# An order of work written out by hand, replaced by another: delta-rule attention and a cosine-gated feed-forward layer on one core

## The chip, the core and the metric

The kernel runs on one core of a Trainium2 chip. The metric is the device time of one execution in microseconds (us); before the change the median of three runs is 665.59 us (663.34 to 668.86). The core has five engines that work side by side, each through its own list of instructions in order: TensorE (PE: matrix products; its weight loads are PEld), VectorE (DVE), ScalarE (ACT), GpSimd (POOL) and SyncE (SP). SP does nothing here but issue transfers (DMAs); ACT issues some too, POOL only the first constants.

## The reference

Two blocks follow each other. The first is a delta rule: for each of 4 batches and 8 heads a 48 x 48 state is carried over 768 tokens. The second is a feed-forward layer on the 3072 tokens, 384 wide, with 2048 hidden features and a cosine gate.

```
k_n = k / (norm(k) + 1e-6)
for t in range(768):
    y[t]  = q[t] @ state
    v_old = k_n[t] @ state
    state = state + beta[t] * outer(k_n[t], v[t] - v_old)
x = y, put together to (3072, 384)
h = x @ w_in ;  out = (h * cos(h)) @ w_out
```

## The kernel before, in words

**Units and pairs.** The 768 tokens are cut into 24 units n of 32 tokens. A unit holds 4 batches x 32 tokens = 128 rows of 8 heads. Two units make a stage m of the attention and a pair p of the feed-forward layer (256 tokens); there are 12 of each.

**Attention, per unit.** Keys and queries are loaded (`k`, `q`, line 327) and turned on PE (`turn`, line 535, and `turn_out`, line 545); from unit 8 on `blocks` (line 338) brings the queries and keys for a turn on DVE (line 551). `square`, `sum`, `norms` (line 487, a power on POOL) and `scale` make the factors; `weigh` scales the values `v`. `gram` (line 566) multiplies keys with keys and queries; `gram_keys`/`gram_queries` (lines 577, 600) take it out; `gram_put` (line 618) writes it to memory and, per stage, `gram_get` (line 639) reads it back with other rows, into the one buffer `gb`. Then the 32 x 32 triangles of the stage are inverted by elimination, `inv(m, 0)` to `inv(m, 6)`: pairs of a product (line 676) and a subtraction (line 683), on POOL (on DVE for stage 0). `put` (line 697) and `get` (lines 708, 716) carry the inverse back. On PE follow `state` (line 733), `solve` (line 796; the first two units solve in halves, `solve_half`, `between`, `solve`), `update` (line 819) and `within` (line 836), with `right`, `solve_out`, `update_out`, `within_out` between them on DVE and ACT; `features` (line 855) hands the unit to the feed-forward layer.

**Weights.** They come as 8-byte floats in 28 pieces (`weights`, line 435), and are cut to 4 bytes by `split` (ACT, lines 443, 445), `shift` (DVE, 449, 454) and `add` (POOL, line 458). `hidden(0, f)` needs the pieces up to 3(f/2 % 4 + 1).

**Feed-forward layer, per pair.** Pairs 0 and 1 take a plain first product, `hidden` (line 876). The others take it in a scheme with fewer products: `x_sum` (line 969, POOL) adds and subtracts blocks of the features into 11 combinations named d, n, m, e, k, g, i, l, f, h and b0 (each 128 x 128); `layer(p, j)` (line 1054) multiplies one with a block of weights, 20 for a pair; `layer_out` (lines 1066, 1068, 1071) combines the results on ACT and DVE. `turns`, `rest`, `cos`, `gate` (lines 917, 924, 933, 936) make h cos(h). The second product is plain for pair 0 (`out`, line 1077); the others take seven products in two parts, `out(p, step, part)` (line 1134), with `left` sums (line 1150) and `collect` (line 1186) on DVE, and a `store`.

**What sets the order.** All of this is added as 2083 tasks with their dependencies. The class `Order` then goes through them in the sequence that the string `LINE` gives, a list of task numbers, and writes out each task's instructions; the costs and due times that `add` also takes are not read. The instructions of an engine run in that sequence, and each waits for what it needs of the others. Buffers follow it too: there is one `gb`, one of the PSUM places named `two` and `kq`, three named `h`. Every transfer issued by SP or ACT waits for the one issued eight places before it in the sequence (the semaphores go round in eight).

In `LINE`, near a change from pair p to the next, the first product with combinations is `layer(p, 18)` (it reads d), then `layer(p, 15)` (no combination), then `layer(p, 1)` (g), `layer(p, 4)` and `layer(p, 10)` (i), with parts of `out(p - 1, ...)` and attention products between them.

Of the kernel before, what the change touches and what calls it, by code (L numbers as in the profile page):

```python
# [55 lines left out]
0 1971 1 2 14 10 11 12 3 4 37 5 42 15 72 6 38 7 39 16 43 73 40 1972 13 1975 44 96 17 75 45 19 97  # L56
18 79 76 46 77 1979 1973 20 48 1976 47 1974 78 80 104 1977 99 1983 100 1978 81 49 101 82 50 83 84
105 102 1987 1984 51 132 106 1980 107 9 108 52 22 1991 131 53 1988 36 54 1995 1981 55 56 155 138
1992 1989 1982 1985 109 1990 1996 1999 1993 1986 139 1997 21 1994 134 41 1998 110 135 818 136 2003
2000 23 57 24 111 2001 25 112 26 2007 27 74 2004 822 28 137 2002 156 29 113 2005 30 2011 186 32 31  # L60
140 33 187 2006 141 114 142 2012 2015 34 98 58 35 2013 210 143 115 59 2016 60 2019 211 679 61 116
2020 2023 241 2021 62 680 63 64 117 2027 65 2024 681 2008 66 2017 68 684 69 265 67 189 118 2009
2031 190 159 103 86 160 685 161 2028 162 2018 119 163 682 2029 70 2014 71 87 2035 2032 193 164 686
2010 683 689 194 2033 85 191 687 688 2039 694 690 825 165 2025 2034 243 820 2030 88 166 244 699
695 2026 2043 89 2036 120 2022 696 691 167 697 90 2037 2040 92 2047 698 719 93 296 91 2044 168
2041 700 701 94 121 702 2048 704 122 2051 2042 703 95 133 692 2045 2038 693 709 245 705 706 2055
192 714 710 157 2049 2046 707 711 2050 708 712 195 2059 169 2052 713 747 8 715 188 196 2056 197
2057 123 748 2063 170 720 826 749 212 124 750 2053 125 2064 198 127 716 2067 320 2058 752 819 717
126 128 2054 2060 751 171 718 129 753 757 2061 130 2068 754 2071 755 2069 214 758 756 2062 762 215
2065 2070 298 158 2066 2075 216 759 247 172 767 217 760 299 763 761 2072 764 2079 2076 772 735 248  # L70
2073 765 173 768 766 145 823 219 773 2077 2080 721 774 269 2081 775 731 777 776 2078 218 174 769
220 2082 146 770 2074 782 268 824 778 771 300 779 722 828 221 144 832 783 833 222 739 723 249 725
724 821 302 246 223 743 147 829 303 726 732 148 834 224 175 784 149 837 151 150 351 727 152 830
780 827 225 736 788 153 176 831 154 785 744 728 737 740 741 226 177 270 242 178 729 179 787 323
733 790 213 227 781 180 793 182 375 181 794 183 838 786 184 796 791 185 840 250 798 842 200 228
251 266 252 789 851 742 799 852 730 792 253 353 201 271 800 272 354 274 855 843 801 745 844 802
856 841 738 229 846 797 845 804 267 847 848 859 849 835 850 275 853 860 355 806 734 857 854 301
868 199 276 273 858 807 869 805 861 304 277 866 862 836 872 357 867 746 202 863 870 203 278 864
230 808 873 865 204 839 206 871 406 876 279 205 207 874 809 795 231 875 803 878 232 877 810 280
324 879 894 882 898 895 233 883 297 899 896 880 234 900 811 881 281 897 358 235 902 237 236 884  # L80
812 430 903 886 885 282 904 208 887 814 209 901 238 325 888 239 815 889 240 905 379 910 954 255
923 953 906 955 816 890 960 907 961 378 408 962 892 911 956 908 922 957 893 958 912 909 959 305
817 283 913 321 918 964 891 968 924 965 306 914 925 307 308 969 919 326 409 920 966 327 813 256
972 329 967 410 921 928 970 915 929 322 971 284 973 979 963 916 931 980 917 330 930 983 933 974
926 331 254 934 927 359 935 285 984 332 981 936 987 413 982 937 411 988 975 932 985 333 412 328
939 976 977 257 941 986 991 258 334 989 992 259 1011 261 260 461 993 262 990 942 1012 335 938 1013
995 940 943 1014 1007 286 944 994 1008 945 336 287 978 946 352 356 996 288 1015 947 999 1009 289
949 337 1010 1016 290 1000 376 1017 292 291 1019 997 948 263 1020 998 485 338 950 380 1021 1001
264 951 293 1003 1002 294 1022 1035 295 1018 1023 1038 1024 1066 360 1004 1041 1068 1025 1005 1069
339 1067 434 1076 1042 1006 1070 361 1073 1031 1077 362 1074 1036 463 1075 1081 1072 1032 363 1078  # L90
1071 381 1026 1082 310 382 1033 383 1027 384 464 1079 1034 1085 465 377 1083 1086 1080 1044 1028
1084 1037 1094 1029 385 1046 1092 1095 309 1087 1030 1093 1039 386 1098 1088 311 952 1096 340 1040
1047 1089 387 1097 1090 1048 1099 1091 312 1102 313 388 1100 414 314 1101 1049 316 468 1043 1104
317 1103 389 315 1050 433 1105 1052 466 1124 1120 341 516 1121 1106 390 342 1122 1108 1054 1107
343 1109 1125 1055 1123 344 1128 467 1110 391 1126 1045 1056 1111 1127 345 1057 347 540 346 1114
1051 392 1112 1129 318 1113 1058 1130 1115 319 1131 1059 348 1136 1053 407 349 1132 1060 393 1118
1137 350 1062 1133 1061 1138 435 1134 1063 1139 489 415 1119 365 1064 1144 1135 518 1116 1179 416
1181 1145 1148 1182 1117 394 1186 1146 418 366 1190 1180 1140 1183 469 1194 1185 1184 1151 417
1195 1189 1141 1187 1147 1188 1198 1142 1149 436 364 1199 1150 1196 1154 1191 437 1143 1207 439
519 1192 1152 1155 520 1193 488 438 1197 1157 1156 1205 1159 440 1153 367 1206 1158 395 1200 368  # L100
1209 1201 1208 522 1160 441 1210 1202 1211 442 1203 1213 1065 523 1161 1204 1214 1212 1217 521 443
431 1215 1218 369 1162 1237 1216 371 571 370 1163 1233 372 444 1234 1165 1238 1164 396 1239 1167
1235 1221 397 490 1168 445 1222 1236 544 1219 1240 398 1220 1223 399 1241 462 1169 1242 446 400
1170 1243 402 1224 401 595 1225 432 1227 373 1226 447 1171 374 1244 403 1228 1245 1172 1166 486
1249 404 1173 1229 405 1246 1231 1250 1292 1174 1294 543 1175 573 1232 1295 1296 1247 1303 1297
574 1293 1176 1302 1304 1262 1298 1251 1248 448 1307 1177 1257 1305 1230 470 1306 1258 420 1308
471 1259 472 1261 421 1260 1264 524 1178 1253 1299 473 575 1252 491 1267 1263 1309 449 492 1268
1254 1310 494 1300 1255 1313 1301 1311 576 578 1314 1318 1312 1256 1270 1265 1319 1266 495 496
1320 1271 419 1322 1272 1315 1273 1323 1316 450 1321 1274 1324 497 1275 577 1317 1326 1269 1276
1327 493 487 1330 498 422 1325 1331 1278 423 1350 1328 1351 424 499 1329 1352 426 626 425 1332  # L110
# [80 lines left out]
def kernel(  # L191
# [159 lines left out]
    near = 132 + C  # L351
# [516 lines left out]
    gates, p_hs, turns, rests, p_os, outs = ({} for _ in range(6))  # L868
# [326 lines left out]
    def store(p, i, cols=slice(0, DM)):  # L1195
# [12 lines left out]
            x=2, x_sum=XS, turns=2, g=GATES, o=2, o_out=2,  # L1208
# [3 lines left out]
    add = order.add  # L1212
# [480 lines left out]
```

## Time and profile before

| | |
|---|---|
| median of three runs | 665.59 us |
| profiled execution: its time / its span | 668.13 us / 666.3 us |
| PE busy / instructions | 604.3 us (91%) / 11960 |
| DVE, POOL, ACT busy | 487.5, 448.5, 261.4 us |
| mean granted TensorE clock | 0.978 |
| DMA: bytes / mean rate | 51.78 MB / 78 GB/s |

The page's second part cuts the span into 40 slices and gives the busy share of each engine in tenths; PEclk is the clock that TensorE was granted. The chain (fourth part) goes back from the last instruction to what released it, step by step. A line of the timeline gives start, duration, engine, source line, operation and tiles, and in brackets the idle time before it and what ended that.

### The profile page before, as it was taken

What the parts mean: (1) busy time and instruction counts of PE and PEld (TensorE: products, weight loads), DVE (VectorE), ACT (ScalarE), POOL (GpSimd) and SP (SyncE); (2) the same over time, 40 slices, a digit from 0 to 9 for tenths busy, and PEclk for the clock granted to TensorE, in tenths of its full rate; (3) what the DMA queues carried; (4) which work ended last, traced back from release to release, by engine and by line L of the source; (5) the groups of instructions that cost most, each with busy time, mean ns of one, the idle gap of its engine ahead of it and who ended that gap; (6) DMA issues with size and microseconds to landing.
All of it is one profiled execution on the core that took longest, in us unless ns stands there. A gap on an engine that the chain in (4) does not pass through costs nothing.

```text
span 666.3 us, 27542 instructions
## 1 busy us (share of the span) xinstructions
PE 604.3 (91%) x11960; PEld 565.6 (85%) x11960; DVE 487.5 (73%) x886; ACT 261.4 (39%) x446; POOL 448.5 (67%) x844
## 2 busy tenths in 40 slices
PE   4317689999989999989999999999999999999997
PEld 3216578896789999989999999998999999999996
DVE  5784275989868888768978778867668678566782
ACT  3432364662123533523533534523334434336340
POOL 4378766888898878858858858968658679403000
PEclk9999698999989999989999999999999999999999
DMA  8875674566353553343453352541421410200000
GB/s 179 195 168 121 157 162 110 129 122 104 58 98 50 77 99 58 55 80 53 78 101 56 72 87 40 93 74 27 72 59 29 86 21 14 47 3 25 1 25 25
DMA packets 215644, 51.78 MB, mean 78 GB/s; under 512 B 207076, under 2 KB 210420, under 8 KB 215524
## 3 DMA queue, kind: packets, MB, share of 16 engines
q1 hardware_dynamic: 204516, 43.39, 35.4%
q10 hardware_dynamic: 10752, 6.20, 3.7%
q8 instruction: 94, 1.54, 1.0%
q0 software_dynamic: 256, 0.44, 0.3%
q14 instruction: 26, 0.21, 0.1%
HBM read 39.24 MB, written 10.75 MB: 75 GB/s over the span
## 4 chain that ended last, share of the span: by engine, by line
PE 45%; POOL 32%; DMA 9%; issue 6%; DVE 4%; ACT 1%; SPq 1%; ACTq 0%; POOLq 0%; DVEq 0%
PE p_out L1134 17%; PE p_h L1054 16%; POOL z L683 13%; POOL part L676 13%; POOL x_sum L969 4%; PE p_h L876 3%; DMA gb<-g_dr 3%; DMA qp<-in_q_dram 2%; PE p_kq L733 2%; PE p_u L796 2%; PE p_o L1134 2%; PE p_s L819 1%; PE p_kq L836 1%; DMA zt<-z_dr 1%; PE p_out L1077 1%
## 5 line engine op out<-in xcount | busy, mean ns | idle before, releaser
L676 POOL TENSOR_TENSOR part<-z,gb 128x126 f32<-128x126 f32 (+22 forms) x341 | 148.8, 436 | 66.6 <-DMA gb<-g_dr 27.0
L683 POOL TENSOR_TENSOR z<-z,part 128x126 f32<-128x126 f32 (+22 forms) x341 | 157.5, 462 | 26.7
L1134 PE MATMUL p_out<-w_out,g_ffn 128*128 128x192 f32 x672 | 120.1, 327 | 0.0
L1134 PEld LDWEIGHTS p_out<-w_out,g_ffn 128*128 128x128 f32 x672 | 107.9, 190 | 0.5
L933 ACT ACTIVATE turns<-turns,halfpi 128x512 f32<-128x512 f32 x96 | 68.7, 721 | 61.3 <-DVE turns L924 60.7
L1134 PE MATMUL p_out<-w_sum,g_ffn 128*128 128x192 f32 x496 | 91.3, 332 | 0.8 <-DVE o L1186 0.8
L1054 PE MATMUL p_h<-x_sum,w_in 128*128 128x128 f32 x640 | 85.5, 282 | 4.2 <-POOL x_sum L969 3.4
L1054 PEld LDWEIGHTS p_h<-x_sum,w_in 128*128 128x128 f32 x640 | 79.2, 195 | 6.0 <-POOL x_sum L969 3.8
L1134 PEld LDWEIGHTS p_out<-w_sum,g_ffn 128*128 128x128 f32 x496 | 80.7, 193 | 1.7 <-DVE o L1186 1.0
L917 ACT ACTIVATE turns<-g_ffn,quarter_turn 128x512 int32<-128x512 f32 x70 | 50.2, 721 | 67.3 <-DVE g_ffn L1071 52.1
L1071 DVE TENSOR_TENSOR g_ffn<-g_ffn,p_h 128x512 f32<-128x512 f32 x80 | 54.4, 682 | 23.8 <-PE p_h L1054 19.6
L1150 DVE TENSOR_TENSOR g_ffn<-g_ffn 128x512 f32<-128x512 f32 x88 | 65.0, 743 | 5.9 <-PE p_out L1134 4.7
L936 DVE TENSOR_TENSOR g_ffn<-turns,g_ffn 128x512 f32<-128x512 f32 x70 | 52.9, 764 | 6.9 <-ACT turns L933 6.8
L924 DVE SCALAR_TENSOR_TENSOR turns<-g_ffn,turns 128x512 f32<-128x512 f32 x70 | 53.1, 767 | 5.9 <-ACT turns L917 5.9
L1054 PE MATMUL p_h<-x_sum,in_sum 128*128 128x128 f32 x400 | 53.8, 279 | 2.3 <-POOL x_sum L969 2.3
L1054 PEld LDWEIGHTS p_h<-x_sum,in_sum 128*128 128x128 f32 x400 | 49.4, 192 | 3.5 <-POOL x_sum L969 2.7
L1186 DVE SCALAR_TENSOR_TENSOR o<-p_out,o 128x192 f32<-128x192 f32 x74 | 25.2, 352 | 34.3 <-PE p_out L1134 33.7
L876 PE MATMUL p_h<-x_ffn,w_in 128*128 128x128 f32 x384 | 48.9, 289 | 0.0
L876 PEld LDWEIGHTS p_h<-x_ffn,w_in 128*128 128x128 f32 x384 | 47.2, 204 | 1.0
L487 POOL TENSOR_TENSOR knrm<-ksum,halves 128x16 f32<-128x16 f32 (+1 forms) x14 | 38.4, 2746 | 10.8 <-DVE ksum L475 10.8
L1054 PE MATMUL p_h<-x_ffn,w_in 128*128 128x128 f32 x320 | 43.7, 280 | 0.0
L1054 PEld LDWEIGHTS p_h<-x_ffn,w_in 128*128 128x128 f32 x320 | 39.2, 191 | 1.1
(122 smaller groups left out, 940.0 us busy)
## 6 DMA issues: line engine op xcount, KB each, us to landing
pairs<-in_moe_w_out_dram SPq DMA_DIRECT2D x13, 384.0 KB
vp<-in_v_dram SPq DMA_DIRECT2D x96, 48.0 KB
gb<-g_dr SPq DMA_DIRECT2D x18, 256.0 KB
out_dram<-o SPq DMA_DIRECT2D x23, 192.0 KB
pairs<-in_moe_w_in_dram SPq DMA_DIRECT2D x7, 512.0 KB
kp<-in_k_dram SPq DMA_DIRECT2D x128, 24.0 KB
z_dr<-z SPq DMA_DIRECT2D x11, 256.0 KB
zt<-z_dr SPq DMA_DIRECT2D x88, 32.0 KB
```

The lines of the kernel that those rows point to most:

```text
L487: nc.gpsimd.tensor_tensor(out=scales[m][2][:, part], in0=sums[m, part.start][:, 0:n], in1=halves[:, 0:n], op=ALU.pow,)
L676: eng.tensor_tensor(out=part, in0=z[:, 0:rows, j, None].to_broadcast(shape), in1=a[:, j, None, j + 1 :].to_broadcast(shape), op=ALU.mult,)
L683: eng.tensor_tensor(out=behind, in0=behind, in1=part, op=ALU.subtract)
L876: nc.tensor.matmul(p_h[:, i], w_in[:, t, (4 * k + i) * 128 : (4 * k + i + 1) * 128], xts[p][:, t, unit * 128 : (unit + 1) * 128], start=(i ...
L917: nc.scalar.activation(turns[p, f], hidden_of(p, f), AF.Identity, bias=quarter_turn, scale=TURN)
L924: nc.vector.scalar_tensor_tensor(out=r, in0=hidden_of(p, f), scalar=TURN, in1=t, op0=ALU.mult, op1=ALU.subtract,)
L933: nc.scalar.activation(r, r, AF.Sin, bias=halfpi, scale=2.0 * math.pi)
L936: nc.vector.tensor_tensor(out=place(p, f), in0=step_of(rests.pop((p, f)), f), in1=step_of(hidden_of(p, f), f), op=ALU.mult,)
L1054: nc.tensor.matmul(p_h[:, e], in_block(*w)[:, e], x_of(p, b), start=new and e == 0, stop=True, skip_group_check=True,)
L1071: nc.vector.tensor_tensor(out=part_of(p, to), in0=part_of(p, one), in1=part_of(p, two), op=op)
L1134: nc.tensor.matmul(p_o, left(p, part, a)[:, e % 4], right(e, b), start=(e == 0), stop=(e == FT // 2 - 1), skip_group_check=True,)
L1150: either(("left", p, x, s), nc.vector, nc.gpsimd).tensor_tensor(out=left(p, s, to), in0=left(p, s, one), in1=left(p, s, two), op=op)
```

## The change

`LINE` is replaced as a whole. Beside it three figures of cost are written anew (a gate's steps, and 0.5 to 0.68 for an `x_sum`); nothing reads them. The 2083 tasks, their instructions, and the engine and the queue that issue them stay the same.

```diff
     LINE = """
-0 1971 1 2 14 10 11 12 3 4 37 5 42 15 72 6 38 7 39 16 43 73 40 1972 13 1975 44 96 17 75 45 19 97
...
-1966 1968 1969 1970
+0 1971 1 2 10 11 12 7 3 37 4 72 14 38 39 42 15 73 1972 13 1975 43 96 1973 97 40 1974 16 44 17 1976
...
+1956 1960 1958 1954 1961 1959 1963 1962 1947 1964 1949 1967 1965 1966 1968 1969 1970
 """
...
+        near = not isinstance(f, tuple) or f == (0, 0, 0)
-        add(("turns", *key), "ACT", 0.73, lambda: hidden_turns(p, f), deps,
+        add(("turns", *key), "ACT", 0.73 if near else 0.76, lambda: hidden_turns(p, f), deps,
...
-            add(("x_sum", p, x), "POOL", 0.5, lambda x=x: x_sum(p, x), deps, other=("DVE", 0.38),
+            add(("x_sum", p, x), "POOL", 0.68, lambda x=x: x_sum(p, x), deps, other=("DVE", 0.42),
```

Of the tasks of PE 408 of 532 stand at another place in its list, of DVE 627 of 696, ACT 333 of 425, POOL 134 of 229, SP 134 of 193. PE's first fifteen tasks (to `gram(4)`) are the same in both. What the lists say at the places that the prediction speaks of:

```
PE, early     before: between1 solve1 update1 within1 hidden(0,2) turn5 state2 gram5 features1 turn6
                      hidden(0,4) hidden(0,6) solve2 hidden(0,8) update2 within2 out(0,0,0) features2
              after:  between1 hidden(0,2) solve1 hidden(0,4) update1 within1 turn5 state2 gram5
                      out(0,0,0) features1 hidden(0,6) turn6 hidden(0,8) solve2 hidden(0,10) update2
SP, early     before: get1 v2 q5 k6 q6 weights11 v3 gram_put4 weights12 q7 weights13 k8 k9 put1
                      weights16 gram_put5 get2 weights18 get3
              after:  v2 get0 weights8 get1 q5 v3 k6 q6 weights11 q7 gram_put4 weights12 v4 weights13
                      k8 v5 weights16 k9 put1 gram_put5 weights18 get2
POOL, inside  before: inv(1): add 7 8          inv(2): add 17 16, norms 4, add 18 19 21 20 22 24 23
an inversion  after:  inv(1): add 8 11 12 13   inv(2): add 18 19 20 22 23 21
PE, pair 2    before: layer(2,18) out(1,2,0) gram9 out(1,2,1) layer(2,15) out(1,3,0) out(1,3,1) layer(2,10)
              after:  out(1,2,0) out(1,2,1) gram9 layer(2,18) layer(2,15) out(1,3,0) out(1,3,1) layer(2,4)
PE, pair 4    before: layer(4,18) layer(4,15) gram13 state10 layer(4,1) layer(4,10) layer(4,4)
              after:  gram13 state10 out(3,0,0) layer(4,18) layer(4,15) out(3,0,1) layer(4,1) layer(4,4)
```

The place of the combinations in POOL's list: how many x_sums of the pair have to be done, and how much PE work of the rows' durations (0.89 us for a layer, 1.30 for a part of out) stands in PE's list between the start of `layer(p, 18)` and the first layer that reads g or i.

```
pair                           2     3     4     5     6     7     8     9    10    11
before: g as number            7     9    11     8     5     7    11     9     9     8
        i as number            6    10    10     7     8    10     9    10     8     9
        PE work before, us   7.8   3.9   3.9   3.1   3.1   3.9   4.4   4.4   4.4   3.1
        x_sums begin         mid   mid   end   end   mid   mid   mid   mid   mid   end
after:  g as number            5     6     5     7     7     6     5     5    10     7
        i as number            7     8     7    10     8     7     8     7    11     6
        PE work before, us   4.4   3.1   3.1   3.1   5.2   4.4   5.2   3.9   4.4   3.1
        x_sums begin         end   mid   end   mid   end   mid   mid   mid   mid   end
(mid: ahead of the last piece of the inversion beside them, inv(m, 6); end: behind it)
```

## The prediction

> **What bounds the kernel now.** I read the page first.
>
> ```profile
> span 666.3 us, 27542 instructions
> ...
> PE 604.3 (91%) x11960; PEld 565.6 (85%) x11960; DVE 487.5 (73%) x886; ACT 261.4 (39%) x446; POOL 448.5 (67%) x844
> ...
> PE   4317689999989999989999999999999999999997
> ...
> POOL 4378766888898878858858858968658679403000
> PEclk9999698999989999989999999999999999999999
> ...
> PE 45%; POOL 32%; DMA 9%; issue 6%; DVE 4%; ACT 1%; SPq 1%; ACTq 0%; POOLq 0%; DVEq 0%
> ```
>
> PE is full from the seventh slice to the end, except in three slices. The instructions do not change, so only two things can: how early PE becomes full, and the dents after that. The busy times by stretch say how large each is (columns: stretch, its length, then PE, PEld, DVE, ACT, POOL busy, the granted clock, DMA share, GB/s).
>
> ```profile
> 60.00:80.00 20.00, 12.56 (x415) 11.29 (x411) 4.03 (x9) 7.32 (x14) 16.80 (x41) 0.68 0.67 152
> 80.00:100.00 20.00, 16.18 (x383) 14.98 (x383) 15.63 (x25) 11.04 (x20) 13.15 (x12) 0.90 0.62 138
> 180.00:200.00 20.00, 17.96 (x355) 17.07 (x354) 13.59 (x30) 4.56 (x8) 18.01 (x34) 0.91 0.48 89
> 280.00:300.00 20.00, 17.71 (x365) 17.16 (x364) 13.68 (x24) 7.19 (x13) 12.68 (x25) 0.91 0.50 89
> 300.00:320.00 20.00, 20.00 (x492) 18.81 (x491) 16.69 (x30) 7.96 (x14) 17.34 (x35) 1.00 0.37 53
> ```
>
> In the two stretches with a dent the clock falls too: 0.91 of 20 us is 1.8 us lost at half clock; the record has it halved for 3.41 us from 186.55 and from 285.54, which is 1.71 us each. The timeline names the dents, with what ended each:
>
> ```profile
> 184.72 0.90 POOL L969 TENSOR_TENSOR x_sum<-x_ffn 128x128 f32<-128x128 f32 x1
> 185.67 1.29 PE L1054 MATMUL p_h<-x_sum,in_sum 128*128 128x128 f32 x8 [2.04 <-POOL x_sum L969]
> ```
>
> ```profile
> 285.71 4.48 PE L1054 MATMUL p_h<-x_sum,w_in 128*128 128x128 f32 x24 [2.29 <-POOL x_sum L969]
> ```
>
> ```profile
> 389.27 1.89 PE L1134 MATMUL p_out<-w_sum,g_ffn 128*128 128x192 f32 x10 [0.82 <-DVE o L1186]
> ```
>
> ```profile
> 479.40 1.16 PE L1054 MATMUL p_h<-x_sum,w_in 128*128 128x128 f32 x8 [1.15 <-POOL x_sum L969]
> ```
>
> So three of four dents are PE at a pair's first layers, waiting for a combination that POOL has not made yet; one more of 0.27 us at 279.43 is of the same kind. They sum to 2.04 + 0.27 + 2.29 + 0.82 + 1.15 = 6.57 us, with the two cold stretches 3.42 more: **10.0 us** that the steady part can give back at most (small idle times of 0.45 to 0.74 us at 157, 173 and 460 left aside).
>
> Ahead of 100 us PE is busy for 51 us only. What holds it there late is a queue:
>
> ```profile
> 74.80 13.60 SPq L327 DMA_DIRECT2D kp<-in_k_dram  x16
> 88.50 0.39 SPq L697 DMA_DIRECT2D z_dr<-z  x1
> ...
> 93.34 1.80 SPq L716 DMA_DIRECT2D zt<-z_dr  x4
> ```
>
> The inversion of stage 1 ends on POOL at 81.19, but its `put` stands behind the loads of k8 and k9, and k9 may not overwrite its keys before `update(1)` has read them (PE, 81.15 to 82.71). From there to `solve(2)`, at 99.57, it takes 16.9 us.
>
> **The start, step by step.** The new sequence has eight more transfers (384 KB) ahead of weights11, whose `split` holds back `half_out(1)`; at the 152 GB/s of that stretch they take 2.6 us, so `between(1)` (74.32 to 75.82) ends at 78.4. Now comes `hidden(0,2)`; the first hidden took 4.63 us at half clock: 83.0. `solve(1)`, 0.9 to 1.5 us: 84.2. `hidden(0,4)`, 2.97 at full clock: 87.2. But `update(1)` also needs `solve_out(1)`, and DVE's list has 7.3 us of work more ahead of that, which ended at 81.0: 88.3. So `update(1)` ends at 89.2, 6.5 later than before. k9 follows as before, and `put(1)`; inversion 1 itself gets two more weight additions (1.0 to 1.3 us each) and is still done by 91, ahead of the `put` at 95.0. So `solve(2)` stands at 106.1. But PE has then done `hidden(0,8)` and `out(0,0,0)` as well, 2.68 and 2.6 us, which it did later before. Net: 6.5 - 5.3 = +1.2. I count **+1.0**, a little being likely to hide in DVE's idle time. From below: were nothing of this later, the 5.3 us would be gained. From above: `put(1)` has ten transfers, 1152 KB, more ahead of it; at 138 GB/s that is 8.5 us, and if all of it came on top, 8.5 + 6.5 - 5.3 = +9.7. I stay near the middle, since both the filled gaps and the longer queue are there.
>
> Behind it POOL gets an easier stage: inside inversion 2 stand six additions (7.5 us of the rows) instead of ten pieces (13.5). That is 6 us in hand for an inversion that starts some 4 us later, so it does not pass the late start on.
>
> **The pairs' beginnings.** A layer takes 0.89 us, a part of out 1.30; an x_sum 0.62 on the mean of 110 rows (68 of them at 0.45 to 0.5, 41 at 0.7 or more). For pair 4 the sequence had g as the eleventh combination and only 3.9 us of PE work ahead of `layer(4,1)`: 10 x 0.62 = 6.2, short by 2.3, which is the 2.29 of the row. The new one has g fifth and 3.1 us of cover: 4 x 0.62 = 2.5, not short; i is seventh: 3.7 against 4.0. For pair 2, `layer(2,18)` moves behind two parts of out and `gram(9)`, 3.5 us, more than the 2.04 that it waited; `x_sum(2,d)` moves behind the last piece of inversion 3, 5.1 us, less what inversions 2 and 3 start sooner. Pair 8 had g eleventh and behind the inversion's last piece, now fifth. The 0.82 at 389 is a part of out for which PSUM had not been cleared; other work stands there now. So all **10.0** go.
>
> **What comes anew.** I set each layer's new place on PE (the sum of the rows ahead of it) against the new place of its combination on POOL. The margin is negative at layers 2,18 (-0.6 us), 4,18 (-0.4), 6,18 (-2.0), 7,3 (-0.4), 9,3 (-0.3) and 10,1 (-1.4): 5.1 together. POOL idled 2 to 6 us before each of the inversions 5 to 9, so it can be sooner than this says; I take half, 2.6, and a quarter of a cold stretch: **+3.0**. Bounds 0 and 5.1 + 1.7. On PE the small and the large products alternate 164 times in both sequences, so that costs nothing new.
>
> At one rule the Trainium skill is against counting the cold stretches. "TensorE: Matmul & The Clock Gate", section "What's actually happening", lets the clock drop after an idle window of some 3.4 us. The rows disagree: idle times of 2.04 and 2.29 us had a cold stretch behind them, those of 0.82 and 1.15 none.
>
> **Sum.** 1.0 - 10.0 + 3.0 = -6.0 against the profiled execution's own 668.13 (span 666.3 and 1.8 around it): 662.1. That execution was 2.5 us above the median of the three shown, 665.59. So **659.6**. Within 1%, 658.9 to 672.2, is about what a measurement can't tell from no change.
>
> **The rivals.**
> - The start comes late: at +9.7 the sum is +2.7, **668.3**. For it: ten transfers more ahead of `put(1)`; against it: DMA was busy only 0.62 of that stretch. Chance 0.15.
> - The start comes early: k9 goes out no later, -5.3, the sum -12.3, **653.3**. For it: PE had 6.6 us of gaps between 71.6 and 81.2, and two hidden products now stand in them; against it: the queue. 0.14.
> - Slower: combinations late at most pairs' beginnings. Each takes what 185.67 took, 2.04 + 1.71 = 3.75. Nine such places (pairs 2 to 10); from five on it decides: 1.0 - 10.0 + 18.75 = +9.75, **675.3**. It happens if x_sums take 0.9 rather than 0.62: then i of pair 4 needs 5.4 against 4.0, g of pair 10 8.1 against 4.4. In the trace the long ones start beside `rest`, `gate` and `left` on DVE (37 of 41), whose operands lie in SBUF; those beside DVE work from PSUM are short. Against it: of six negative margins only one is over 1.5. 0.17. The Trainium skill, "GPSIMD Engine Reference", section "Key points", has GpSimd and VectorE contend for SBUF when a VectorE instruction has two SBUF inputs; the trace agrees, 0.9 us against 0.46.
> - The waits are only moved, +10.0 instead of +3.0: the new sequence does not do what it is meant to. **666.6**, 0.07.
> - The clock does not fall for waits this short (the rule of the Trainium skill, above): 3.4 us are not there to gain, **663.0**. 0.02.
> - The forecast, 653 to 666: 0.45, of which 0.22 below 658.9.
>
> Faster by over 1%: 0.22 + 0.14 = 0.36; within: 0.23 + 0.15 + 0.07 + 0.02 = 0.47; slower: 0.17. The range for 8 in 10 reaches from 650 (a start at -5.3 with no new waits gives 650.3) to 675 (the slow rival).
>
> **What would show it.** `solve(2)` near 106, with two hidden products between `between(1)` and `update(1)`; `put(1)` behind k9 at 95. No idle time over 1.2 us before a layer at pairs 2, 4 and 8, granted clock 1.00 from 110 us on. It is wrong if the waits for x_sum on PE (5.7 us before) do not shrink to half, or if PE fills only after 110 us.

## The result, and the profile after

The median after the change is 661.35 us (11 runs, 657.69 to 667.34), before it 665.78 (11 runs of the same occasion, 663.34 to 668.86). The ratio is **0.994, with a 95% interval of 0.9915 to 0.9965**: faster by 4.4 us, which is within 1%. The profiled execution of after took 659.55 us (span 657.8), 1.8 below its median; that of before 668.13, 2.4 above its own. So the traces are 8.6 us apart where the medians are 4.4 apart: what is read below from one trace against the other holds some 4 us of chance, and the experiments, which are timed, decide.

The page of after, with the lines that answer to those of before:

```profile
span 657.8 us, 27560 instructions
...
PE 598.3 (91%) x11960; PEld 561.2 (85%) x11960; DVE 485.7 (74%) x886; ACT 259.7 (39%) x446; POOL 448.2 (68%) x844
...
PE   3316889989989999999999999899999999999997
...
POOL 4458698878888888868968848868688589203000
PEclk9999799989999999999999999999999999999999
...
PE 52%; POOL 23%; DMA 10%; SPq 5%; issue 5%; DVE 4%; ACT 1%; ACTq 0%; POOLq 0%; DVEq 0%
```

PE has an 8 in the fifth slice where it had a 6. Later on it had an 8 in the slices from 183 and 283 us; now in those from 132, 181 and 411. On the chain POOL's share falls from 32% to 23%, and that of SP's queue rises from 1% to 5%. The busy times by stretch (columns as before: stretch, length, PE, PEld, DVE, ACT, POOL, clock, DMA share, GB/s):

```profile
60.00:80.00 20.00, 14.91 (x469) 13.56 (x465) 9.16 (x16) 6.66 (x13) 14.58 (x28) 0.74 0.63 150
80.00:100.00 20.00, 17.11 (x411) 14.99 (x400) 16.89 (x28) 12.65 (x25) 18.21 (x24) 1.00 0.70 166
140.00:160.00 20.00, 17.92 (x159) 14.70 (x160) 16.74 (x27) 6.47 (x11) 15.55 (x25) 0.91 0.60 100
180.00:200.00 20.00, 18.19 (x247) 17.48 (x247) 14.69 (x32) 5.64 (x10) 16.48 (x34) 1.00 0.60 100
280.00:300.00 20.00, 19.99 (x471) 18.91 (x471) 15.13 (x25) 7.11 (x12) 13.18 (x30) 1.00 0.59 95
```

Between 60 and 100 us PE is busy for 32.0 us (28.7 before) at a higher clock (0.74 and 1.00 for 0.68 and 0.90). The dent of pair 4, at 285, is gone. That of pair 2, at 185, is there without the cold clock, and there is a new one at 142 with it.

To place the difference I use a **loss**: the time at which a PE task ends, less the work of all PE tasks up to it, each at one fixed duration (0.89 us a layer, 1.30 a part of out, 2.68 a hidden, and so on). What the loss grows by in a stretch is what PE lost there, whatever the sequence.

| loss, us, at | 85 | 105 | 130 | 200 | 300 | end |
|---|---|---|---|---|---|---|
| before | 61.2 | 64.8 | 66.9 | 73.0 | 78.8 | 85.9 |
| after | 56.5 | 60.4 | 60.8 | 67.7 | 71.5 | 77.3 |

So 6.1 of the 8.6 us between the traces come from the start, and 2.5 from everything behind 130 us.

The timeline of after has the start as follows (SPq is SP's queue of transfers):

```profile
73.80 0.46 ACT L772 COPY u_half<-p_w 128x384 f32<-128x384 f32 x1
75.73 0.88 PE L762 MATMUL p_v<-u_half,halves_z 32*32 32x48 f32 x64
76.54 2.94 PE L875 MATMUL p_h<-x_ffn,w_in 128*128 128x128 f32 x24
...
80.23 2.94 PE L875 MATMUL p_h<-x_ffn,w_in 128*128 128x128 f32 x24
83.10 0.89 PE L818 MATMUL p_s<-u,kp 64*64 64x96 f32 x32
84.37 5.53 SPq L326 DMA_DIRECT2D kp<-in_k_dram  x8
89.16 0.23 POOL L682 TENSOR_TENSOR z<-z,part 128x16 f32<-128x16 f32 x1
90.51 1.16 SPq L696 DMA_DIRECT2D z_dr<-z  x1
94.54 2.53 SPq L715 DMA_DIRECT2D zt<-z_dr  x4
101.16 1.03 PE L795 MATMUL p_u<-rhs,zt 32*32 32x48 f32 x58 [0.34 <-DMA zt<-z_dr]
```

The first two lines are `half_out(1)` and `between(1)`, which needs it. Before, `half_out(1)` ended at the same time, and PE stood waiting for it:

```profile
73.80 0.47 ACT L773 COPY u_half<-p_w 128x384 f32<-128x384 f32 x1
74.32 1.50 PE L763 MATMUL p_v<-u_half,halves_z 32*32 32x48 f32 x64 [2.76 <-ACT u_half L773]
```

In after the two hidden products stand around `solve(1)`, at 2.94 us each; `update(1)` ends at 84.0, k9 goes out behind it and `put(1)` behind k9. The POOL line is the end of inversion 1, at 89.39. `solve(2)` starts at 100.5 (its first four products; the row shows the rest), 1 us later than before, with 5.2 us more of PE's work done (41.8 for 36.6 us at its end). The largest new wait of the steady part is a chain through three engines:

```profile
140.20 1.00 POOL L457 TENSOR_TENSOR w_out<-w_out,pairs 128x384 uint32<-128x384 uint32 x1
141.24 0.69 DVE L935 TENSOR_TENSOR g_ffn<-turns,p_h 128x512 f32<-128x512 f32 x1 [3.86 <-POOL w_out L457]
142.08 5.10 PE L875 MATMUL p_h<-x_ffn,w_in 128*128 128x128 f32 x29 [2.27 <-DVE g_ffn L935]
```

DVE's `gate(1,6)` stood for 3.86 us until POOL's addition of weight piece 24 had ended, and PE's `hidden(1,10)` for the gate (its row runs on into the next hidden product); a cold stretch follows (142.86 to 146.27, 1.71 us lost). The code tells why. Gates and weight loads share eight tiles. When `gate(1,6)` comes, all eight are held: by four gates, and by the pieces 24 to 27, of which 24 is given back by an `add` that stands behind the whole of `inv(2, 6)` in POOL's list. The other waits of after that exceed 0.9 us behind 130:

```profile
185.42 1.16 PE L1053 MATMUL p_h<-x_sum,in_sum 128*128 128x128 f32 x8 [1.50 <-POOL x_sum L968]
...
272.83 0.89 PE L732 MATMUL p_kq<-st,kq_t 48*32 48x48 f32 x72 [0.98 <-issue]
...
422.05 1.16 PE L1053 MATMUL p_h<-x_sum,w_in 128*128 128x128 f32 x8 [1.74 <-POOL x_sum L968]
```

### The profile page after: what moved, and what is told of

Same layout as the page of the kernel before. It is cut to its first block, busy times and chain, and to the rows that moved or that the text cites. A ratio compares the mean times of both kernels' runs of the same rounds, so it can differ in the third digit from the quotient of the medians.

```text
span 657.8 us, 27560 instructions
## 1 busy us (share of the span) xinstructions
PE 598.3 (91%) x11960; PEld 561.2 (85%) x11960; DVE 485.7 (74%) x886; ACT 259.7 (39%) x446; POOL 448.2 (68%) x844
## 3 DMA queue, kind: packets, MB, share of 16 engines
q8 instruction: 94, 1.54, 1.0%
## 4 chain that ended last, share of the span: by engine, by line
PE 52%; POOL 23%; DMA 10%; SPq 5%; issue 5%; DVE 4%; ACT 1%; ACTq 0%; POOLq 0%; DVEq 0%
PE p_out L1133 19%; PE p_h L1053 19%; POOL part L675 10%; POOL z L682 10%; PE p_h L875 3%; DMA qp<-in_q_dram 3%; PE p_kq L732 2%; DMA gb<-g_dr 2%; PE p_u L795 2%; PE p_s L818 2%; PE p_kq L835 2%; PE p_o L1133 2%; DMA g_dr<-g 1%; DMA pairs<-in_moe_w_in_dram 1%; POOL x_sum L968 1%
## 5 line engine op out<-in xcount | busy, mean ns | idle before, releaser
L675 POOL TENSOR_TENSOR part<-z,gb 128x126 f32<-128x126 f32 (+22 forms) x341 | 154.0, 452 | 57.2 <-DMA gb<-g_dr 15.4
L682 POOL TENSOR_TENSOR z<-z,part 128x126 f32<-128x126 f32 (+22 forms) x341 | 155.4, 456 | 26.7
L1133 PE MATMUL p_out<-w_sum,g_ffn 128*128 128x192 f32 x496 | 89.1, 329 | 0.3 <-issue 0.3
L932 ACT ACTIVATE turns<-turns,halfpi 128x512 f32<-128x512 f32 x96 | 68.3, 720 | 47.0 <-DVE turns L923 46.8
L1053 PE MATMUL p_h<-x_sum,w_in 128*128 128x128 f32 x640 | 83.2, 278 | 1.7 <-POOL x_sum L968 1.7
L1053 PEld LDWEIGHTS p_h<-x_sum,w_in 128*128 128x128 f32 x640 | 77.3, 192 | 3.5 <-POOL x_sum L968 2.1
L916 ACT ACTIVATE turns<-g_ffn,quarter_turn 128x512 int32<-128x512 f32 x70 | 50.4, 720 | 55.9 <-DVE g_ffn L1070 37.2
```

The lines of the kernel that those rows point to most:

```text
L675: eng.tensor_tensor(out=part, in0=z[:, 0:rows, j, None].to_broadcast(shape), in1=a[:, j, None, j + 1 :].to_broadcast(shape), op=ALU.mult,)
L682: eng.tensor_tensor(out=behind, in0=behind, in1=part, op=ALU.subtract)
L916: nc.scalar.activation(turns[p, f], hidden_of(p, f), AF.Identity, bias=quarter_turn, scale=TURN)
L932: nc.scalar.activation(r, r, AF.Sin, bias=halfpi, scale=2.0 * math.pi)
L1053: nc.tensor.matmul(p_h[:, e], in_block(*w)[:, e], x_of(p, b), start=new and e == 0, stop=True, skip_group_check=True,)
L1133: nc.tensor.matmul(p_o, left(p, part, a)[:, e % 4], right(e, b), start=(e == 0), stop=(e == FT // 2 - 1), skip_group_check=True,)
```

## The experiments

Each was timed beside the kernel before; a ratio is to that, with its 95% interval. Source lines are those of after; `two_hidden`, `dents_old` and `stalls` have them one or two higher.

### Which half of the order does it: start_new and rest_new

```diff
 start_new: LINE =
+  after's sequence up to update(2)            (262 tasks)
   before's sequence for all the other tasks
 rest_new:  LINE =
   before's sequence up to update(2)           (241 tasks)
+  after's sequence for all the other tasks
```

> The new order up to update(2) (262 tasks), and behind it what is left in the old order. Theory A: the gain is made ahead of 131 us, where TensorE's time less the work done fell from 66.9 to 60.8 us in the two traces; then this kernel gains about 6 us on the kernel before, 660 against 666, and its trace has the waits of 2.0 and 2.3 us for x_sum at pairs 2 and 4 again. Rival B (the prediction's sum): the start costs 1.0 and the gain is in the steady part; then it stands at 666 to 667.

> The old order up to update(2) (241 tasks), and behind it what is left in the new order. Theory A: only what the two traces differ by behind 131 us, 2.5 us, so about 663. Rival B: the steady part alone is worth 7.0, so about 659, with no wait for x_sum over 1.2 us.

**start_new: 660.95 us, 0.9906 [0.9872, 0.9941]. rest_new: 666.53 us, 0.9992 [0.9967, 1.0017].** The whole gain is in the new start (6.3 us by the ratio; 6.0 by its loss at 130 us, 60.9). The new rest, some 1800 tasks of it, gains nothing that can be measured; on the new start it may even cost something, for after's ratio is 0.994, but the intervals overlap. In start_new the old dent of pair 4 is back; that of pair 2, which I also expected, is not:

```profile
277.73 2.50 PE L1053 MATMUL p_h<-x_sum,w_in 128*128 128x128 f32 x10 [2.29 <-POOL x_sum L968]
```

In rest_new pair 4 has no wait for a combination (1.00 us there, at `state(10)`, is PE's wait for its own instructions), but that of pair 2 is larger than in either kernel:

```profile
192.98 1.16 PE L1053 MATMUL p_h<-x_sum,in_sum 128*128 128x128 f32 x8 [2.54 <-POOL x_sum L968]
```

### What in the start: two_hidden and start_no_out

```diff
 two_hidden (before):  between(1) +hidden(0,2) solve(1) +hidden(0,4) update(1) within(1)
-                      hidden(0,2) turn5 ... turn6 hidden(0,4)
+                      turn5 ... turn6
 start_no_out (start_new):
-  state2 gram5 out(0,0,0) features1 ... update2 within2
+  state2 gram5 features1 ... update2 within2 out(0,0,0)
```

> The kernel before with two tasks moved: hidden(0,2) right behind between(1), hidden(0,4) right behind solve(1). Theory A1: filling the two waits of 2.59 and 1.24 us is what made the start faster: 3.8 us less, and up to 5 more if the clock rises sooner, so 657 to 662. Theory A2: the two products only move; update(1) comes some 2 us later, solve(2) too, and TensorE waits behind update(1), where nothing else is ready: 665 to 668. The weights and the out part that the new order also brings forward are then what the gain needs.

> start_new (the new order up to update(2), the old one behind it) with out(0,0,0) put back behind within(2), where the old order has it. Theory F: what counts ahead of solve(2) is how much ready work TensorE has while k9, put(1) and the loads behind it run (16.5 us in both traces); then 2.9 us go back, ratio 0.995, as in two_hidden, and an idle time of 2 to 3 us stands ahead of solve(2). Rival G: the gain was made ahead of 85 us by the two hidden products alone; then 0.991 stays.

**two_hidden: 665.14 us, 0.9970 [0.9949, 0.9992]. start_no_out: 665.16 us, 0.9965 [0.9945, 0.9985].** The two hidden products alone bring the loss at 85 us to 56.2, as good as after's 56.5. But 7 us are lost again up to 105 (63.0; after loses 3.9 there), and 2 us of gain are left. What keeps the gain in the new start is `out(0,0,0)` ahead of `features(1)`: with it put back, the loss at 95 us is 62.3 (start_new 57.1). The timeline of start_no_out has the two places:

```profile
89.89 0.68 PE L732 MATMUL p_kq<-st,kq_t 48*32 48x48 f32 x49 [2.01 <-issue]
...
93.33 0.87 PE L854 MATMUL p_z<-consts,y 128*128 128x128 f32 x3 [2.08 <-DVE tt L599]
```

The second is `features(1)` waiting for DVE, whose list is long by then. In start_new `features(1)` stands at 91.15 without a wait, behind the 2.85 us of `out(0,0,0)`. That one move is worth 0.9965 - 0.9906 = 0.0059, or 3.9 us: most of the new start's 6.3. The intervals of the two just don't meet; they come from two occasions, each beside the kernel before. In the traces it is not the wait alone: start_no_out has a half clock from 92.85 to 96.27 us, start_new has none there, and 2.08 us of wait and 1.71 of cold clock make 3.8. Theory F had the size about right, but no wait stands ahead of `solve(2)`.

### Can the dents be had without the new order: dents_old and start_sums

```diff
 dents_old (before):  x_sum(4, ..) in the order
-  as before, with g as number 11 and i as number 10
+  d m e k g n i b0 l f h
-  layer(2,18) out(1,2,0)
+  out(1,2,0) layer(2,18)
 start_sums (start_new):
+  the same order for pair 4; x_sum(8,g) behind x_sum(8,k)
```

> The kernel before with the two large waits of its steady part taken away: at pair 4 the combinations k, g and i are made earlier on GpSimd, at pair 2 layer(2,18) stands behind out(1,2,0). If each wait is worth what the trace shows with its cold stretch (2.29 + 1.71 and 2.04 + 1.71, some 0.5 left at pair 2), it gains 7.2 us: 658.5. If the clock's part is not real: 3.8 us, 662. If such waits only move to the next place: 0, 666.

> start_new (the new order up to update(2), the old one behind it) with the combinations of pair 4 made in the order d, m, e, k, g, n, i, b0, l, f, h on GpSimd, as in dents_old, and g of pair 8 made behind k, ahead of inversion 9's last piece. In start_new's trace TensorE waits 2.29 us (and 1.71 of cold clock) for g of pair 4 and 1.42 us for g of pair 8; neither stands behind a long piece of an inversion alone, so GpSimd has the time. Theory: both waits go, 3.7 to 5.4 us: ratio to the kernel before 0.983 to 0.985 against start_new's 0.991. Rival: they come back at the next pairs, as at pair 2 of dents_old: 0.990.

**dents_old: 665.38 us, 0.9964 [0.9934, 0.9995]. start_sums: 662.19 us, 0.9922 [0.9895, 0.9949], no better than start_new.** Of the 7.2 us that I expected of dents_old came 2.4 (0.0036 of 667.5). Pair 4's wait is gone there (0.77 us of issue is left), and `layer(2,18)`, with a part of out of 1.30 us ahead of it, waits for 0.17 us only; but a later layer of the same pair, `layer(2,10)`, waits for longer than `layer(2,18)` had, with a cold stretch behind it:

```profile
194.21 4.57 PE L1054 MATMUL p_h<-x_sum,w_in 128*128 128x128 f32 x24 [2.69 <-POOL x_sum L969]
```

In start_sums pair 4's wait for a combination is gone too (1.11 us of issue stands at `layer(4,10)`), and pair 8's falls from 1.42 to 1.09 us. Further on three waits for combinations are new, 1.20 us at pair 5, 0.55 and 1.58 at pair 9; two of them:

```profile
326.00 1.16 PE L1053 MATMUL p_h<-x_sum,w_in 128*128 128x128 f32 x8 [1.20 <-POOL x_sum L968]
...
525.38 1.16 PE L1053 MATMUL p_h<-x_sum,in_sum 128*128 128x128 f32 x8 [1.58 <-POOL x_sum L968]
```

So a dent that is mended is not its own length of gain: the time comes back at a later layer or pair.

### The wait at 142 us: tile_free and mended

```diff
 tile_free (after):
-  weights27 where it stands
+  put(2) weights27
 mended (after): tile_free's move, and
+  gram_get(3) right behind put(2), ahead of weights27
+  norms(5,0) ahead of add(26)
+  x_sum(2,d) ahead of inv(3,6), inv(3,6) behind features_out(5)
+  x_sum(7,i) ahead of inv(8,6)
+  gram13 ahead of layer(3,16)
```

> The new order with one load moved: weights27 goes out behind put(2) instead of ahead of it, so that one of the eight tiles which the gates share with the loads is free when gate(1,6) wants one. In the trace of the new order gate(1,6) waits 3.9 us on VectorE until GpSimd's addition of weights24 has ended, and hidden(1,10) on TensorE 2.3 us behind it, with a cold stretch. Theory T: it waits for the tile that this addition gives back; then this kernel's gate(1,6) follows its cosine without the wait, and 4.0 us are gained at 142 us (2.27 and 1.71): ratio to the kernel before 0.988, of which up to 2.5 may be lost again at pair 2, where GpSimd sets the time. Rival: the wait is for something else on GpSimd's list; then the wait and the ratio, 0.994, stay.

> The new order with six moves: gram_get(3) and then weights27 right behind put(2), norms(5,0) ahead of two weight additions on GpSimd, x_sum(2,d) ahead of the last piece of inversion 3, x_sum(7,i) ahead of the last piece of inversion 8, gram(13) two places from state(10). They aim at the waits of 2.27 (with 1.71 of cold clock), 1.50, 1.74 and 0.98 us. Theory P: TensorE's waits are worth their sum, 8.2 us: ratio 0.982. Theory Q: GpSimd's chain of inversions sets when the pairs begin, and only what it gains counts, 2.9 us at 147 (gram_get ahead of the queries' loads) and some of the later ones: ratio 0.986 to 0.990, with waits for x_sum at pairs 2 and 3 in the place of those taken away.

**tile_free: 663.42 us, 0.9952 [0.9931, 0.9973]. mended: 666.34 us, 0.9984 [0.9961, 1.0007].** In tile_free the gate goes through without a wait, which settles the eight tiles as the cause. But the kernel is no faster than after. Piece 27 now comes late (1.29 us at 146.95), and pair 2 waits for longer:

```profile
137.95 0.67 DVE L935 TENSOR_TENSOR g_ffn<-turns,p_h 128x512 f32<-128x512 f32 x1
...
185.15 0.23 POOL L682 TENSOR_TENSOR z<-z,part 128x16 f32<-128x16 f32 x1
185.33 0.45 POOL L968 TENSOR_TENSOR x_sum<-x_ffn 128x128 f32<-128x128 f32 x1
...
185.84 1.60 PE L1053 MATMUL p_h<-x_sum,in_sum 128*128 128x128 f32 x8 [4.33 <-POOL x_sum L968]
```

The first POOL line is the end of inversion 3, the second `x_sum(2,d)` right behind it. The inversion runs from 150.4 to 185.4 us here, from 150.3 to 185.0 in after. PE came 2.4 us sooner and met the same end. For mended both theories on record missed (0.982; 0.986 to 0.990). The named waits nearly go (0.53 at pair 2, 0.71 at pair 7), and others stand in their place: the largest behind the late piece 27, and one for issue at `state(10)`, from which `gram13` was moved away (0.98 in after):

```profile
149.97 4.54 PE L875 MATMUL p_h<-x_ffn,w_in 128*128 128x128 f32 x24 [3.30 <-DVE g_ffn L935]
...
278.18 0.89 PE L732 MATMUL p_kq<-st,kq_t 48*32 48x48 f32 x72 [2.51 <-issue]
```

### Past the combinations: dve_sums and chain

```diff
 dve_sums (tile_free): seven combinations of pair 2 made by DVE, d behind features_out(5), six behind left(1,2,1)
     OTHER = {
...
-        ('weights', 10), ('weights', 14), ('weights', 15), ('weights', 17)
+        ('weights', 10), ('weights', 14), ('weights', 15), ('weights', 17),
+        *(('x_sum', 2, x) for x in 'dmekgni')
 chain (after): the same seven on DVE, and
+  shift(24) and add(24) ahead of inv(2,6);  gram_get(3) right behind put(2)
+  x_sum(7,i) ahead of inv(8,6)
```

> tile_free with the combinations d, m, e, k, n, g, i of pair 2 made on VectorE, behind features_out(5) and left(1,2,1), and not on GpSimd behind inversion 3. Theory Q: GpSimd's inversion 3, which runs from 150.4 to 185.4 in both traces whatever TensorE has gained, is what layer(2,18) waits for; then the 4.33 us at 185 and the cold clock behind them go, 4 to 6 us: ratio 0.986 to 0.989 against tile_free's 0.995. Rival: the layer would wait for something else as long (features, the tiles of the layers): 0.995 stays.

> The new order with four things mended on GpSimd's chain: the addition of weights24 (and VectorE's shift for it) ahead of inversion 2's last piece, so that gate(1,6) finds its tile at 136 us; gram_get(3) right behind put(2) on SyncE, ahead of four loads of queries; d, m, e, k, n, g, i of pair 2 on VectorE as in dve_sums; x_sum(7,i) ahead of the last piece of inversion 8. Unlike mended, no load of weights is put off. Theory Q: inversions 2 to 5 on GpSimd set the pace until some 290 us, and a wait of TensorE that goes while they stay where they are comes back at the next place; here inversion 3 starts 2 to 3 us sooner (147.5 against 150.3), so most of the waits at 142, 185 and 422 (7.2 us with the cold clock) are gained: 3 to 6 us, ratio 0.985 to 0.989 against 0.994. Rival P: waits taken away in the steady part come back in any case, as in tile_free, mended and start_sums: 0.992 to 0.996.

**dve_sums: 661.62 us (4 runs), 0.9896 [0.9857, 0.9934]. chain: 660.78 us, 0.9935 [0.9914, 0.9957].** dve_sums comes near the 0.986 to 0.989 of its theory, and its interval leaves out tile_free's 0.995; but the two intervals touch, and there are four runs. Its wait at 185 is gone, but `hidden(1,14)` waits 2.78 us at 147 behind the late piece 27, with a cold stretch. In chain the waits at 142 and 185 are gone, that of pair 7 is 0.99 us, and inversion 3 runs from 146.9 to 182.1. The three waits that it aims at are gone or nearly halved, and the ratio is after's: it lies in the rival's band, 0.992 to 0.996. In both kernels `solve(6)` now waits, for the result of the same inversion 3; the timelines of dve_sums and of chain:

```profile
197.01 1.56 PE L795 MATMUL p_u<-rhs,zt 32*32 32x48 f32 x64 [2.07 <-DMA zt<-z_dr]
```

```profile
192.96 1.50 PE L795 MATMUL p_u<-rhs,zt 32*32 32x48 f32 x64 [2.49 <-DMA zt<-z_dr]
```

No kernel of the study is faster than after, or than start_new, by more than the intervals allow.

### Two rules by themselves: stalls and grams

Both are after with work added, for the trace alone. stalls makes the combination d of pairs 3 to 10 several times over, so that PE waits for it; grams makes three of the gram products several times over.

```diff
 stalls:
+        for _ in range({3: 16, 4: 12, 5: 12, 6: 6, 7: 13, 8: 8, 9: 12, 10: 9}.get(p, 1) if x == "d" else 1):
             either(("x_sum", p, x), nc.gpsimd, nc.vector).tensor_tensor(
 grams:
-        for j in range(NP):
+        for j in [*range(NP)] * {15: 2, 17: 4, 21: 8}.get(n, 1):
```

> The new order with x_sum(p,d) of pairs 3 to 10 written 6 to 16 times over (the same values again), which holds back layer(p,18) by some 1.5 to 3.5 us at each of the eight pairs. Theory W: TensorE's clock is set for stretches of 3.41 us one after the other, by how much of the stretch before TensorE was idle; in the traces so far 2.04 us or more of one stretch had a half clock behind them, 1.86 us or less had none, and an idle time of 2.0 to 2.5 us that lies across the border of two stretches had none either. Then of these eight those that lie across a border stay without. Rival V: the length of the idle time alone decides, 2.0 us and more are followed by a cold stretch wherever they lie. Rival S: only idle times over 3.4 us are.

> The new order with the 64 products of gram(15) written twice, of gram(17) four times, of gram(21) eight times (the same values again, so the result is the same). One gram is 128 instructions of TensorE (64 weight loads, 64 products) in 0.86 us. Theory I: TensorE reads its instructions in pieces of 16 KB, 256 instructions, and where it runs dry a piece counts from the start of its transfer to 1.3 us behind its landing, some 2.4 us; then eight grams take not 6.9 us but 8 to 9, with idle times of 0.5 to 1 us that end 1.3 us behind a landing on its instruction queue. Rival: the waits at state(1), state(2) and state(10) had other causes; then the eight follow each other in 6.9 us.

**stalls: 699.63 us.** The waits made range from 1.4 to 5.4 us. Four of them in the timeline:

```profile
337.27 2.94 PE L1054 MATMUL p_h<-x_sum,w_in 128*128 128x128 f32 x24 [2.47 <-POOL x_sum L969]
...
386.23 1.16 PE L1054 MATMUL p_h<-x_sum,in_sum 128*128 128x128 f32 x8 [3.49 <-POOL x_sum L969]
...
539.03 1.22 PE L1054 MATMUL p_h<-x_sum,in_sum 128*128 128x128 f32 x4 [3.82 <-POOL x_sum L969]
...
590.41 2.08 PE L1054 MATMUL p_h<-x_sum,in_sum 128*128 128x128 f32 x8 [3.61 <-POOL x_sum L969]
```

The granted clock goes in stretches of 3.41 us whose borders do not move with the work. The 2.47 us at 337 are cut by a border into 1.69 and 0.78: no cold stretch, and the 24 products take 2.94 us. The 3.49 at 386 are cut into 1.53 and 1.95: a cold stretch follows the second part. So in these cases it is the idle time inside one stretch that counts, theory W on record, and not the length of the wait. At 539 and 590 a cold stretch has 1.16 and 1.34 us of the wait in it, and the one behind it is cold too.

**grams: 683.26 us.** The products of one gram eight times over take 12.4 us for 6.9, with a pause each 3.74 us that nothing in the program asks for:

```profile
470.31 1.80 PE L565 MATMUL p_g<-kq_t 48*32 48x64 f32 x143
473.40 1.47 PE L565 MATMUL p_g<-kq_t 48*32 48x64 f32 x128 [1.28 <-issue]
477.14 2.04 PE L565 MATMUL p_g<-kq_t 48*32 48x64 f32 x128 [2.28 <-issue]
480.89 1.84 PE L565 MATMUL p_g<-kq_t 48*32 48x64 f32 x113 [1.71 <-issue]
```

Between pauses stand 128 products, which with their weight loads are 256 instructions. The transfers show a piece of 16 KB for PE's instructions landing at 472.05, 475.71 and 479.42; PE goes on 1.35, 1.43 and 1.47 us behind each. So a long run of small products outruns the reading of its own instructions. I had expected 8 to 9 us; a part of the 12.4 is a half clock, from 474.97 us on.

## Why the prediction came out as it did

It said 659.6 us, in 650 to 675; the median is 661.35, and the gain, forecast at 6.0 us, is 4.4. The size was right, and **the reasons were not**: the start was put 7 us too dear, the rest 4.5 too cheap in the traces (some 6.5 by rest_new), and the two nearly cancel.

- **What bounds the kernel.** That only the filling of PE and the dents can move the time fits: all 8.6 us are in the loss, as by its definition they must be. That the queue on SP holds the start late holds in part only. `put(1)` goes out at 90.51, 0.6 us behind the last transfer of k9 (to 89.90); what it waited for last was the transfer eight places before it, a piece of weights that landed at 90.45. But inversion 1 itself, with four additions inside it and a wait of 3.61 us ahead of one of them, ended at 89.39 (81.19 before): without the queue `put(1)` could have gone out 1.1 us sooner, where it was 7.3 before.
- **The start, +1.0 (bounds -5.3 to +9.7): wrong, -6.1** in the trace, -6.3 by the timing of start_new. It lies just under the lower bound, and is what the rival "the start comes early" described. That rival went by k9 being no later; k9 was later, `put(1)` by 2.0 us and `solve(2)` by 1.0. Three terms were mis-sized and one was missing:
  - `between(1)`, put 2.6 us later for eight transfers, ended at 76.6 rather than 78.4, 0.8 us later than before, and not for the transfers: weights11 went out 1.0 us later (68.53 for 67.50), but its `split` began at 72.68 (72.69 before) and `half_out(1)` ended at 74.26 (74.27). What it had to wait for was PE: `hidden(0,0)` began 4.4 us later (71.29 for 66.93), behind waits of 2.29 us for issue at `state(1)` and 2.20 at `solve_half(1)` (0.37 and 0.69 before), and filled the time that PE had stood idle.
  - `hidden(0,2)`, counted at the cold 4.63 us, took 2.94. In before the clock is half from 73.91 to 84.15, that is, while PE waits there; in after it is full from 74.59 on. I took a row's duration from a place where PE was idle for a place where the change makes it busy.
  - DVE's 7.3 us of work more ahead of `solve_out(1)` was counted whole. DVE was busy for 4.03 of the 20 us from 60 to 80, as the quoted row said, and is now for 9.16: most of it went into idle time, and `solve_out(1)` ended at 82.9 rather than 88.3.
  - The 5.3 us of work brought forward was right: 5.2. But `out(0,0,0)`, 2.6 of it, also covers the wait of `features(1)` for DVE, and with it saves a cold stretch; the move is worth 3.9 us by the timing of start_new and start_no_out, and the sum, which set all of the 5.3 against a later `update(1)`, had no term for a cover.
- **Inversion 2 easier by 6 us: low.** It took 46.8 us before and takes 37.2 now (102.9 to 140.1), for the additions of weights went forward into POOL's gaps (busy 18.21 for 13.15 us from 80 to 100). It starts at 102.9 in both, not some 4 us later, so whether it would pass a late start on was not put to the test.
- **The old dents, -10.0: -8.5.** Those of pairs 4 and 8, at 279 and at 389, are gone with both cold stretches. Pair 2 still waits, 1.50 for 2.04. `layer(2,18)` moved back by 3.5 us of PE's work, but `x_sum(2,d)` moved behind the end of inversion 3, and I took it that inversions 2 and 3 would start sooner by enough.
- **New waits, +3.0 (0 to 6.8): 7.6 without pair 2's.** Of my six negative margins only `layer(2,18)` became a wait, and the five others had time in hand or just none to wait (0.05 us at pair 10, 0.26 and 0.34 at pairs 6 and 7, 1.89 at pair 9, 3.32 at pair 4). The new waits came where I had set up no margin: `hidden(1,10)` behind the eight tiles (2.27 and 1.71 cold), `layer(7,4)` behind `inv(8,6)` on POOL (1.74), PE's own instructions (0.98), and two of 0.50 and 0.42. Of a buffer whose return stands behind an inversion on another engine, the sum had no term.
- **"That costs nothing new"** of the 164 alternations: wrong as put. The number of alternations does not count, but where a piece of instructions ends does. Waits of `state` for issue were 0.4 us before and are 5.1 after (2.29, 1.87 and 0.98), most of it in the start, and so inside its -6.1.
- **The sum of the steady part** was -7.0. It is -2.5 in the loss, of which -10.0 + 9.1 are named waits and 1.6 us small idle times that I don't place. rest_new puts it at nothing, so even the 2.5 may be chance.
- **The rivals.** "Slower, combinations late at most beginnings" needed an x_sum of 0.9 us; the mean stayed 0.61, and the wait came at two beginnings, not five. "The waits are only moved" (+10.0 for the new ones) had 0.07 and is close to what the steady part did: 9.1, and nothing by the timing. "The clock doesn't fall for waits this short" is half right, below.
- **What would show it.** Right: two hidden products between `between(1)` and `update(1)` and `put(1)` behind k9, which the lists alone settle, and no wait over 1.2 us at pairs 4 and 8. Wrong: `put(1)` at 95 (90.5), `solve(2)` near 106 (100.5, against 99.57 before), pair 2's wait, a clock of 1.00 from 110 on (one cold stretch at 142.86). The waits for x_sum fell from 5.7 to 3.2 us, not to half, which I had set as a sign of being wrong, and rightly.

**Why mended dents don't pay.** Up to pair 2 the end of inversion 3 on POOL seems to set the pace. Over the twelve traces from before to chain the loss at 200 us goes with it; eight of them:

| | before | rest_new | two_hidden | start_sums | tile_free | after | start_new | chain |
|---|---|---|---|---|---|---|---|---|
| inversion 3 ends, us | 191.2 | 192.5 | 188.6 | 186.4 | 185.4 | 185.0 | 184.1 | 182.1 |
| loss at 200, us | 73.0 | 75.1 | 69.3 | 67.5 | 69.6 | 67.7 | 65.0 | 65.8 |

The correlation over all twelve is 0.93, at some 0.9 us of loss for each microsecond. In after's order `layer(2,18)` waits for it or, where that is freed, `solve(6)`; in the old order `x_sum(2,d)` is made ahead of that end, and in start_new neither of the two waits. This is argued, not shown: no run moved the inversion alone, a faster start could bring both numbers down without the one causing the other, one execution stands for each kernel, and chain has the earliest end without the best ratio. In its trace the lead is kept to the end (span 655.4 us, after 657.8), but that execution was 3.5 us below its median, and the timings show no lead. Why stays open.

## What to carry to other kernels

Where PE has idle time early, put independent products ahead of each instruction that waits, and cost their neighbours' later work by the idle time on the engines that carry it, not by its own length; and read the duration of a product that fills a gap from a row at full clock. Before a wait deep in the steady part is mended, look for the producer that sets its end: if that end stays, the time comes back at the next one that needs it. When an order is moved, follow the shared buffers as well, and ask behind which instruction of another engine the last one is given back.

## What the runs showed of the hardware

**When the clock falls.** In the traces of all these kernels, behind 110 us and among products of 128 x 128, an idle time of 1.95 us or more within one stretch of 3.41 us had a half-clock stretch behind it (twelve cases, 1.95 to 3.4), and one of 1.13 to 1.79 had none (nineteen cases). Waits of 2.03, 2.29, 2.47 and 2.54 us cut by a border had none either. The half clock stayed for another stretch where that had 0.71 us or more of idle time (0.71 in start_no_out, 1.15 and 1.33 in stalls), and lifted where it had 0.5 or less. Where the stretch has a run of small products in it less was enough at times, 1.26 us in dve_sums, 1.41 in chain, 1.58 in start_no_out, and at times not: 1.48 and 1.53 in tile_free, 1.54 in stalls. What decides there is open. The same wait of 2.29 us at pair 4 was cold in before and in start_new and not in two_hidden, where the products behind it took 2.94 us:

```profile
282.01 2.94 PE L1054 MATMUL p_h<-x_sum,w_in 128*128 128x128 f32 x24 [2.29 <-POOL x_sum L969]
```

So the 1.71 us of a cold stretch behind a wait of 2 to 3.5 us is partly luck, and the 3.4 us that the prediction counted for two of them was too.

The Trainium skill, "TensorE: Matmul & The Clock Gate", section "What's actually happening", has a free-running window of 3413 ns: the stretches of 3.41 us agree, and that they do not move with the work as well. Its section "Why this matters for your kernels" asks for no idle gaps on PE over some 3 us; here 1.95 us in one stretch was enough.

**PE's own instructions.** PE reads them in pieces of 16 KB, 256 instructions; the page of after counts 94 pieces, 1.54 MB, for 11960 products and as many weight loads. Every idle time of 0.4 us or more that the timeline ends by "issue" (58 in the fourteen traces) ends 1.26 to 1.65 us behind the landing of such a piece, three of them 1.9 to 2.2. In after three of them stand at `state(1)`, `state(2)` and `state(10)`; the first two:

```profile
65.48 0.96 PE L732 MATMUL p_kq<-st,kq_t 48*32 48x48 f32 x57 [2.29 <-issue]
...
88.98 0.67 PE L732 MATMUL p_kq<-st,kq_t 48*32 48x48 f32 x49 [1.87 <-issue]
```

The pieces landed at 64.09 and 87.66 us, 1.39 and 1.32 us ahead of them. In every kernel with the new start these two stand at the same tasks, so the place in PE's list seems to decide; the waits over 0.9 us stand in runs of small products or shortly behind them.
